# Normalising the second half's x in pieces during the first half, and giving its first column of h to the rounds of seven products

## The chip, the cores and the metric

One Trainium2 chip, one of its cores. The time is the device time of one execution in microseconds (us), as the median over several runs; the profile is of one execution, taken by the hardware profiler. Engines are called PE (TensorE: matmuls), PEld (its weight loads, which overlap), DVE (VectorE), ACT (ScalarE), POOL (GpSimd) and SP (SyncE, whose queue issues nearly all DMAs here).

## What is computed

x is 2048 tokens by 576 features. The reference normalises it, adds a spectral filter of it and a gated MLP with 4608 hidden columns:

```python
x = A_x
xn = _layernorm(x, axis=-1)
return x + _A_ref(xn, A_w_r, A_w_i) + _B_ref(xn, B_w_gate, B_w_up, B_w_down)
# _A_ref: irfft2(rfft2(xn) * (w_r + 1j * w_i))
# _B_ref: (sigmoid(xn @ w_gate) * (xn @ w_up)) @ w_down
```

All of it is fp32 in effect: each factor of a product is split into a high and a low part in the matmul format fp32r, and three of the four partial products are summed.

## The kernel before

**Halves and units.** The tokens are worked in two halves p = 0, 1 of 1024 tokens (two chunks of 512, or 8 tiles of 128). The hidden columns are worked in 36 blocks f of 128; unit u = 36p + f computes gate and value of block f for the tokens of its half. The first two units of each half (0, 1, 36, 37) are plain products, called in four calls by unit and chunk. All others use a scheme of seven products instead of eight: each product is 7 matmuls of 128x512 (`made`, L710) into the banks pA, pB and pE, from seven-scheme factors of x in the SBUF tensor `X` (A11, A12, A21, A22 and their sums S1 to S4) and factors of the weights in `w`. After a product into pE, DVE adds it to the value (`ys`, L814 for chunk 1, called y1 here, and L834 for chunk 0, y0) and multiplies by the gate (L836). The next product into the same bank waits for the first of these.

**The weights.** The first half reads the raw weights, makes sums and low parts of them (L282 on ACT; L284, L286, L306 to L309 on DVE) and spills seven sections per unit to DRAM (`wsp`). The second half reads them back, each section of 320 KB (L323) into the one place that the product of the unit before has just left, so a section has six products' time to land.

**h times w_down.** Two neighbouring blocks make a column j of h (18 columns). Of the two ways to multiply it, the plain one is `down` (L860, po): 12 matmuls of 128x288 for one tile, 8 tiles, so 96 for a column, then an addition to `acc` (L869). The other is the round (`seven`, L1071, ps): it takes two columns at once through seven items (factors `hs` of h, `wf` of w_down) of two steps with 12 matmuls of 128x288, so 168 a pair; its sums are L1005. A single column in a round is 84. `TWOS` lists which columns go through rounds: in the first half the pairs [2,3] to [14,15], in the second half the pairs [1,2] to [13,14], and [15] alone. Columns 0, 16 and 17 of the second half (0, 1, 16 and 17 of the first) are plain. A unit has seven turns; at each the next step of a round, or a `down`, and the side work is emitted. The eight `down`s of the second half's column 0 stand at turns 3 to 6 of unit 38 (`spots`), and the rounds of the second half begin at turn 5 of unit 41. From unit 39 on the spectral branch's passes are emitted there too (pd and others, L527 and on).

**The boundary.** Around units 34 to 37 x of the second half must be normalised into `X`. `second_pair` and `second_chunk_of_pair` read it transposed (`xg`), with rows of means and reciprocal deviations broadcast (`mr`), and `level` subtracts and multiplies on DVE (L1307, L1308); `second_factors` makes the sums of blocks (L1368); `put` writes high parts on ACT (L1357, L1358) and low parts on DVE (L1359, L1360) into `X`, where each factor may be overwritten only once the last unit of the first half has used it. The statistics come from `later_stats`, one tile in every fourth unit.

The order of instructions on each engine is set by a scheduler from the order of the code and its dependences; each engine then runs its own row in order, so an instruction that waits holds up all that stand behind it on its engine.

Of the kernel before, what the change touches and what calls it, by code (L numbers as in the profile page):

```python
# [16 lines left out]
P = 128  # L17
# [122 lines left out]
def _layout(x, w_r, w_i, w_gate, w_up, w_down):  # L140
# [10 lines left out]
    xg = x.reshape(NT, P, 2, HD)[TPP:, ..., ks].reshape(2, TPC, P, 2, KT + 1, P).transpose(0, 3, 5, 4, 1, 2).reshape(2, 2, P, (KT + 1) * CW)  # L151
# [12 lines left out]
def spectral_glu_kernel(ctx: ExitStack, tc: tile.TileContext, x, xt, xg, ri, w_in, w_down, out):  # L164
# [35 lines left out]
    rowd = tc.dram_tile([2, NT, P], F32, name="rowd")  # L200
# [142 lines left out]
    def parts_d(f):  # L343
        j, g = divmod(f, G)
        st, w = STD[j][:, g], flat(new_f((0, j, g), f"wd{f}"))
        placed(nc.scalar.activation(w[:, 0], st, AF.Copy))
        yield
        nc.vector.tensor_tensor(w[:, 1], st, f32(w[:, 0]), op=OP.subtract)
        if j not in SEVEN:
            nc.sync.dma_start(wdsp[f], f32(w).rearrange("p a d -> p (a d)"))  # L350
        else:
            for b in range(2):
                if (g, b) != (0, 1):
                    nc.sync.dma_start(fsp[j][:, WHERE[f"B{g + 1}{b + 1}"]], f32(w[:, :, b * HD:(b + 1) * HD]))
        yield
# [6 lines left out]

    def make_t(j):

        b = STD[j].rearrange("p g (b d) -> p (g b) d", b=2)
        t = R["pool"].tile([P, 4, HD], F32, tag="xa", name=f"wt{j}", bufs=TPC)
        nc.vector.tensor_tensor(t[:, 1:3], b[:, 1::2], b[:, :2], op=OP.subtract)
        yield
        nc.vector.tensor_tensor(t[:, 3], b[:, 3], t[:, 1], op=OP.subtract)
        nc.vector.tensor_tensor(t[:, 0], b[:, 2], t[:, 3], op=OP.subtract)  # L370
        yield
        th, tl = (R["pool"].tile([P, 4, HD], F32R, tag="xa", name=f"{k}{j}", bufs=TPC) for k in ("wth", "wtl"))
        nc.scalar.activation(th, t, AF.Copy)
        yield
        nc.vector.tensor_tensor(tl, t, f32(th), op=OP.subtract)
        for i, v in enumerate((th, tl)):
            nc.sync.dma_start(fsp[j][:, WHERE["T4"]:WHERE["T4"] + 4, i], f32(v))
        yield

    def make_dt(j):  # L380
# [9 lines left out]
        if j in SEVEN:  # L390
            yield from make_t(j)
# [451 lines left out]
    def down(p, j, m, together=True):  # L843
# [18 lines left out]
        def add():  # L862
# [91 lines left out]
    def split_rows(j, g):  # L954
# [7 lines left out]
        nc.sync.dma_start(wdsp[G * j + g].rearrange("p (a b d) -> p a b d", a=2, b=2), f32(w))  # L962

# [51 lines left out]
    def seven(p):  # L1015
# [9 lines left out]
        last = TWOS[p][-1] if p == 0 else TWOS[p][-2]  # L1025
# [34 lines left out]
        for i, (n, mm) in enumerate(steps):  # L1060
# [12 lines left out]
            slow = len(js) == 2 and js is not last  # L1073
# [256 lines left out]
    def load_whole(h):  # L1330
        t = R["pool"].tile([P, 4, 3, P], F32, tag="raw", name=f"xg1_{h}", bufs=2)
        t = t.rearrange("p b k f -> p (b k f)")
        nc.sync.dma_start(t, xg[1, h])
        WHOLE[h] = t = t.rearrange("p (k s) -> p k s", s=CW)
        XG[1, h], XGR[1, h] = t[:, :KT], t[:KR, KT]
# [247 lines left out]
```

## Time and profile before

| | us |
| --- | --- |
| median of 3 runs | 1370.13 (1370.08 to 1373.65) |
| profiled execution | 1369.23 |
| its span | 1367.4 |
| PE busy | 1356.0 (99%) |
| DVE busy | 1068.2 (78%) |
| ACT busy | 781.0 (57%) |

The span is from the first to the last instruction that the profiler records; the execution is 1.8 us longer than that. The busy times of the engines overlap. PE's granted clock is 1.00 nearly throughout, its higher level of 2.4 GHz. A matmul's own time in the trace is longer than the distance to the next one, since they are pipelined: a group of back-to-back matmuls is read by its length over its count.

### The profile page before, as it was taken

How to read it: one execution, taken by the hardware profiler on the slowest of the kernel's cores; microseconds unless marked ns; L12 is line 12 of the kernel's file. 1: busy time of each engine (PE TensorE's matmuls, PEld its weight loads, DVE VectorE, ACT ScalarE, POOL GpSimd, SP SyncE). 2: the span in 40 equal slices, each digit the busy share in tenths (PEclk: the TensorE clock that was granted, in tenths of full speed). 3: DMA queues.
4: the chain of work that ended last, by engine and by line, in shares of the span. 5: the costliest groups of instructions: out<-in, count | busy, mean ns of one | idle time of the engine just before them, and what ended most of it. 6: DMA issues, size and time to landing. Idle time of an engine off the chain costs nothing.

```text
span 1367.4 us, 20360 instructions
## 1 busy us (share of the span) xinstructions
PE 1356.0 (99%) x7656; PEld 1201.1 (88%) x7656; DVE 1068.2 (78%) x1555; ACT 781.0 (57%) x1228; POOL 3.3 (0%) x5
## 2 busy tenths in 40 slices
PE   8999999999999999999999999999999999999998
PEld 6888888888888888988888999988888888899887
DVE  7978988887878787999458768668777847777886
ACT  6644667676767677843236545447767634444442
POOL 0000000000000000000000000000000000000000
PEclk9999999999999999999999999999999999999999
DMA  7567877767676776585878887799898787775643
GB/s 260 210 227 279 301 292 267 275 262 273 263 268 263 276 264 267 206 311 184 302 246 267 267 252 249 215 307 314 301 311 304 241 282 243 239 232 178 200 150 87
DMA packets 127058, 346.56 MB, mean 253 GB/s; under 512 B 12816, under 2 KB 34096, under 8 KB 122224
## 3 DMA queue, kind: packets, MB, share of 16 engines
q1 hardware_dynamic: 125968, 343.94, 72.5%
q8 instruction: 61, 1.00, 0.3%
q10 hardware_dynamic: 992, 1.31, 0.3%
q14 instruction: 37, 0.30, 0.1%
HBM read 208.74 MB, written 136.46 MB: 252 GB/s over the span
## 4 chain that ended last, share of the span: by engine, by line
PE 95%; DVE 3%; issue 1%; ACT 0%; DMA 0%; DVEq 0%
PE pB L710 24%; PE ps L1071 24%; PE pE L710 17%; PE pA L710 16%; PE po L860 6%; PE pd L527 2%; PE pe L650 2%; PE pa L543 1%; PE pc L591 1%; PE py L619 1%; PE pb L566 1%; PE pz L632 0%; DVE w L284 0%; DVE X L477 0%; PE pg L710 0%
## 5 line engine op out<-in xcount | busy, mean ns | idle before, releaser
L710 PE MATMUL pB<-X,w 128*128 128x512 f32 x1484 | 374.9, 391 | 0.2 <-DVE X L477 0.2
L1071 PE MATMUL ps<-wf,hs 128*128 128x288 f32 x2436 | 358.6, 295 | 0.5 <-DVE acc L1005 0.4
L1071 PEld LDWEIGHTS ps<-wf,hs 128*128 128x128 f32 x2436 | 341.7, 188 | 14.9 <-ACT u L593 1.9
L710 PEld LDWEIGHTS pB<-X,w 128*128 128x128 f32 x1484 | 271.0, 188 | 49.1 <-DVE X L477 0.6
L710 PE MATMUL pE<-X,w 128*128 128x512 f32 x1064 | 265.3, 391 | 1.1 <-DVE ys L834 1.0
L710 PE MATMUL pA<-X,w 128*128 128x512 f32 (+1 forms) x1006 | 252.8, 389 | 0.7 <-DVE X L1359 0.3
L710 PEld LDWEIGHTS pE<-X,w 128*128 128x128 f32 x1064 | 194.1, 188 | 37.3 <-issue 1.4
L710 PEld LDWEIGHTS pA<-X,w 128*128 128x128 f32 x1006 | 182.6, 188 | 33.7 <-ACT X L476 0.7
L992 DVE TENSOR_TENSOR hs<-ys,hs 128x1024 fp32r<-128x1024 f32 (+1 forms) x105 | 124.7, 1187 | 35.8 <-ACT hs L989 34.4
L989 ACT ACTIVATE hs<-ys 128x1024 fp32r<-128x1024 f32 (+1 forms) x105 | 108.0, 1029 | 41.5 <-PE ps L1071 25.6
L282 ACT ACTIVATE w<-raw 128x768 fp32r<-128x768 f32 (+1 forms) x106 | 100.2, 948 | 25.7 <-DVE raw L306 8.6
L836 DVE TENSOR_TENSOR ys<-ys,g 128x1024 f32<-128x1024 f32 x67 | 81.9, 1223 | 3.6 <-DVE ys L834 0.5
L803 ACT ACTIVATE v<-pB 128x512 f32<-128x512 f32 x68 | 40.5, 596 | 76.2 <-PE pB L710 75.8
L284 DVE TENSOR_TENSOR w<-raw,w 128x512 fp32r<-128x512 f32 (+1 forms) x106 | 81.7, 771 | 2.9 <-ACT w L282 2.8
L817 ACT ACTIVATE g<-pB 128x512 f32<-128x512 f32 x68 | 40.6, 597 | 67.7 <-PE pB L710 67.3
L985 DVE TENSOR_TENSOR ys<-ys 128x1024 f32<-128x1024 f32 (+1 forms) x60 | 71.1, 1186 | 0.7
L860 PEld LDWEIGHTS po<-wb,hp 128*128 128x128 f32 x468 | 65.0, 188 | 3.0 <-DVE acc L869 0.4
L860 PE MATMUL po<-wb,hp 128*128 128x288 f32 x468 | 67.3, 295 | 0.0
L814 DVE TENSOR_TENSOR ys<-v,pE 128x512 f32<-128x512 f32 x68 | 46.5, 684 | 26.3 <-ACT v L809 26.0
L1005 DVE TENSOR_TENSOR acc<-acc,ps 128x576 f32<-128x576 f32 x55 | 41.2, 750 | 31.8 <-PE ps L1071 31.4
L834 DVE TENSOR_TENSOR ys<-v,pE 128x512 f32<-128x512 f32 x67 | 45.9, 684 | 23.6 <-PE pE L710 22.4
L869 DVE TENSOR_TENSOR acc<-acc,po 128x576 f32<-128x576 f32 x55 | 41.0, 751 | 23.9 <-PE po L860 23.7
(185 smaller groups left out, 1586.8 us busy)
## 6 DMA issues: line engine op xcount, KB each, us to landing
w<-wsp SPq DMA_DIRECT2D x246, 320.0 KB, 4.0
wsp<-w SPq DMA_DIRECT2D x34, 2240.0 KB, 6.8
wf<-fsp SPq DMA_DIRECT2D x105, 288.0 KB, 4.3
fsp<-wf SPq DMA_DIRECT2D x98, 288.0 KB, 3.4
raw<-in_w SPq DMA_DIRECT2D x34, 768.0 KB, 6.6
x<-sc SPq DMA_DIRECT2D x16, 580.0 KB, 5.5
ri<-in_ri SPq DMA_DIRECT2D x16, 580.0 KB, 5.6
dt<-in_wd SPq DMA_DIRECT2D x32, 288.0 KB, 5.2
```

Of the source, the lines that this page charges most:

```text
L282: placed(nc.scalar.activation(o[:, :, :3, :], src, AF.Copy))
L284: placed(nc.vector.tensor_tensor(o[:, :, 3:, :], src[:, :, :KT, :], f32(o[:, :, :KT, :]), op=OP.subtract))
L710: strictly(nc.tensor.matmul(bank[:, cols], w[:, sw, :], X[:, x, sx, cols], start=start and j == 0, stop=stop and j == len(steps) - 1, skip ...
L814: nc.vector.tensor_tensor(y1, v[:, 1], bank["E"], op=OP.add)
L834: nc.vector.tensor_tensor(place(u, 0), v[:, 0], bank["E"], op=OP.add)
L836: nc.vector.tensor_tensor(h, h, g, op=OP.mult)
L860: nc.tensor.matmul(pd[b], l, r, start=start, stop=stop)
L985: nc.vector.tensor_tensor(o, at(a), at(b), op=op)
L989: nc.scalar.activation(hs[:, :, 0], o, AF.Copy)
L992: nc.vector.tensor_tensor(hs[:, :, 1], o, f32(hs[:, :, 0]), op=OP.subtract)
L1005: nc.vector.tensor_tensor(o, a, b, op=op)
L1071: nc.tensor.matmul(pd[:, s], h[:, g, a, m], w[:, g, b], start=q == 0 and not seeded, stop=q == len(parts_) - 1, skip_group_check=seeded)
```

## The change

Three things are changed.

1. `TWOS[1]` is now [0,1] to [14,15], eight pairs. Column 0's `down`s in unit 38 and the lone [15] are gone; the rounds of the second half begin at turn 5 of unit 39. The factors of w_down for columns 0 and 1 that earlier came from `make_t` are made by `first_sums` in the second half's first units: it reads four pieces of w_down, sums them on DVE, splits four tiles `wt_T` on ACT and DVE and writes eight times 288 KB to `fsp`, from which the round reads them.
2. In the first half, 12 pieces of the second half's x (128 features of 4 x 128 tokens, 256 KB) are read in units 14 to 16, 18 to 20, 22 to 24 and 26 to 28. For each, `piece_level` issues four DVE instructions of 128x256 and `piece_sums`, a unit later, four of 128x128; the piece is written to the DRAM tensor `nsp` after each of the two. The statistics for it are moved to units 4 to 11, and one broadcast read per group of three pieces brings them in.
3. At the boundary the eight factors are read whole from `nsp` (`staged`, 768 KB each) and only `put` is left. The `acc` tiles of the second half are loaded at the turns of unit 38 (`new_acc`) instead of right after each spill.

The core of the diff:

```diff
+FIRST = LATE + 10
+SEVEN = range(NF // G - 2)
+PAIRED = [list(SEVEN[i:i + 2]) for i in range(0, len(SEVEN), 2)]
+TWOS = (PAIRED[1:], PAIRED)
...
-        if j in SEVEN:
-            yield from make_t(j)
...
-                    new_acc(1, m)
...
+    def first_sums():
+
+        js = TWOS[1][0]
+        for _ in range(4):
+            yield
+        for g in range(G):
+            load_raw_d(js, g)
+            yield
+        yield
+        yield
+        for i in range(2):
+            sums_d(js, i)
+            yield
+        sub_d(js, "T4", "B21", "T2", "B11")
+        for nm in ("T4", "T1", "T3", "T2"):
+            w = new_f((1, nm), f"wt_{nm}")
+            nc.scalar.activation(w[:, :, 0], d(js, nm), AF.Copy)
+            nc.vector.tensor_tensor(w[:, :, 1], d(js, nm), f32(w[:, :, 0]), op=OP.subtract)
+            for i, j in enumerate(js):
+                nc.sync.dma_start(fsp[j][:, WHERE[nm]], f32(w[:, i]))
+            yield
...
-        last = TWOS[p][-1] if p == 0 else TWOS[p][-2]
+        last = TWOS[p][-1]
...
-        for h in range(2):
-            level(0, XG[0, h])
-            yield
-            level(0, XGR[0, h])
-            yield
...
+    def piece_level(n):
+        v, b = ROWS2[n // (KT + 1)], PIECE[n]
+        for i, op in enumerate((OP.subtract, OP.mult)):
+            for c in range(2):
+                tc.keep_in_program_order(nc.vector.tensor_tensor(b[:, c], b[:, c], v[:, c, i].unsqueeze(1).to_broadcast([P, 2, P]), op=op))
+
+    def piece_sums(n):
+        A11, A12, A21, A22 = (PIECE[n][:, c, h] for c in range(2) for h in range(2))
+        for o, a, b, op in ((A22, A21, A22, OP.add), (A21, A11, A21, OP.subtract), (A11, A22, A11, OP.subtract), (A12, A12, A11, OP.subtract)):
+            tc.keep_in_program_order(nc.vector.tensor_tensor(o, a, b, op=op))
+
+    def piece_out(n, first):
+        m, k = divmod(n, KT + 1)
+        nc.sync.dma_start(nsp[first:first + 4, :, k, m * P:(m + 1) * P].rearrange("a p s -> p a s"),
+                          PIECE[n].rearrange("p c h s -> p (c h) s"))
...
+    def second_rows():
+
+        staged("A22", True)
+        yield
+        put("A11")
+        staged("S1")
...
-        both(A22, A21, A22, OP.add)
-        yield
-        put("S1", *A22)
...
+    for n in range(TPC * (KT + 1)):
+        q, r = divmod(n, 3)
+        u = FIRST + 4 * q + r
+        at, then = (u, (4, 4, 5)[r]), (u + 1, (4, 5, 6)[r])
+        for (u, i), f, *a in ((later_step(*at, -3), piece_in), (at, piece_level), (later_step(*at, 1), piece_out, 0),
+                              (then, piece_sums), (later_step(*then, 1), piece_out, 4)):
+            behind.setdefault((u, i), []).append(lambda f=f, n=n, a=a: f(n, *a))
...
+    for m in range(TPP):
+        extra.setdefault((NF + G + m // 7, m % 7), []).append(lambda m=m: new_acc(1, m))
...
-            if u == NF + G:
-
-                spots = {3: 2, 4: 2, 5: 2, 6: 2}
-            elif f == NF - 2:
+            if f == NF - 2:
...
-            if p == 0 and f and f % 4 == 0:
-                sides.append(later_stats(TPP + f // 4 - 1))
+            if LATE <= u < LATE + TPP:
+                sides.append(later_stats(TPP + u - LATE, (4, 5, 3, 4)[u % 4]))
```

What it does to the rows of the engines is shown at three places. First DVE in the first half, unit 26, from the adding of w_down pieces (dt) to the first weight work of the next unit; hs and wf are the factors of the round, ys<-v,pE the two additions y1 and y0. Before:

```order
L930 TENSOR_TENSOR dt<-dt 128x2x288
L814 TENSOR_TENSOR ys<-v_4155,pE_4157 128x512
L992 TENSOR_TENSOR hs_10_6_4304<-ys,hs_10_6_4304 128x2x512
L941 TENSOR_TENSOR wf_10_6_4306<-dt,wf_10_6_4306 128x2x288
L834 TENSOR_TENSOR ys<-v_4155,pE_4157 128x512
L930 TENSOR_TENSOR dt<-dt 128x2x288
L836 TENSOR_TENSOR ys<-ys,g_4154 128x2x512
L284 TENSOR_TENSOR w_4327<-raw_4308,w_4327 128x3x256
```

and after, with pc the piece and mr the statistics for it:

```order
L911 TENSOR_TENSOR dt<-dt 128x2x288
L796 TENSOR_TENSOR ys<-v_4297,pE_4299 128x512
L1314 TENSOR_TENSOR pc_4350<-pc_4350,mr_4347 128x256 x4
L997 TENSOR_TENSOR hs_10_6_4457<-ys,hs_10_6_4457 128x2x512
L922 TENSOR_TENSOR wf_10_6_4459<-dt,wf_10_6_4459 128x2x288
L816 TENSOR_TENSOR ys<-v_4297,pE_4299 128x512
L911 TENSOR_TENSOR dt<-dt 128x2x288
L818 TENSOR_TENSOR ys<-ys,g_4296 128x2x512
L287 TENSOR_TENSOR w_4480<-raw_4461,w_4480 128x3x256
```

The four instructions on a piece stand between y1 and the low part of hs; nothing else moved here.

Second, DVE at the boundary, from the last of the work on xg to y0 of unit 35. Before:

```order
L1307 TENSOR_TENSOR xg_1_5686<-xg_1_5686,mr_5683 128x1536
L961 TENSOR_TENSOR wb_17_0_5786<-dt,wb_17_0_5786 128x576
L1308 TENSOR_TENSOR xg_1_5686<-xg_1_5686,mr_5683 128x1536
L1359 TENSOR_TENSOR X<-xg_1_5506,X 128x1024
L1360 TENSOR_TENSOR X<-xgr,X 32x512
L814 TENSOR_TENSOR ys<-v_5689,pE_5691 128x512
L961 TENSOR_TENSOR wb_17_1_5796<-dt,wb_17_1_5796 128x576
L1359 TENSOR_TENSOR X<-xg_0_5509,X 128x1024
L1360 TENSOR_TENSOR X<-xg_0_5509,X 32x512
L1359 TENSOR_TENSOR X<-xg_1_5686,X 128x1024
L1360 TENSOR_TENSOR X<-xg_1_5686,X 32x512
L834 TENSOR_TENSOR ys<-v_5689,pE_5691 128x512
```

and after, where x_A are the factors read whole (A12, A21 and A22 in this order; that of S1 comes just ahead of the first row):

```order
L1341 TENSOR_TENSOR X<-x_A_5650,X 128x1024
L851 TENSOR_TENSOR acc<-acc,po_7_5890 128x576
L883 TENSOR_TENSOR hp_17_0_5903<-ys,hp_17_0_5903 128x512
L942 TENSOR_TENSOR wb_17_0_5916<-dt,wb_17_0_5916 128x576
L1342 TENSOR_TENSOR X<-x_A_5650,X 32x512
L796 TENSOR_TENSOR ys<-v_5821,pE_5823 128x512
L942 TENSOR_TENSOR wb_17_1_5928<-dt,wb_17_1_5928 128x576
L1341 TENSOR_TENSOR X<-x_A_5652,X 128x1024
L1342 TENSOR_TENSOR X<-x_A_5652,X 32x512
L1341 TENSOR_TENSOR X<-x_A_5818,X 128x1024
L1342 TENSOR_TENSOR X<-x_A_5818,X 32x512
L816 TENSOR_TENSOR ys<-v_5821,pE_5823 128x512
```

The instructions on xg (L1307, L1308) are gone, and y0 still stands behind the low parts of A21 and A22, which are now read from x_A.

Third, SP's queue around units 38 and 39. The loads of unit 39's weights are those from wsp_76 before and from wsp_77 after, those of unit 40 from wsp_77 and wsp_78. Before:

```order
L323 DMA w_6055<-wsp_75 128x640 x6
L323 DMA w_6055<-wsp_76 128x640
L172 DMA cf<-c_cf 128x2900
L323 DMA w_6055<-wsp_76 128x640 x4
L502 DMA xs_6364<-in_xt 128x768
L323 DMA w_6055<-wsp_77 128x640
L172 DMA am_6366<-c_am 128x512
L502 DMA xs_6413<-in_xt 128x768
L172 DMA am_6415<-c_am 128x512
L323 DMA w_6055<-wsp_76 128x640 x2
L968 DMA wf_1_0_6730<-fsp_145 128x576
L968 DMA wf_1_0_6730<-fsp_146 128x576
```

and after:

```order
L376 DMA acc<-in_x 128x576 x4
L326 DMA w_6178<-wsp_77 128x640
L966 DMA fsp_146<-wt_T_6304 128x576
L326 DMA w_6178<-wsp_77 128x640
L966 DMA fsp_147<-wt_T_6304 128x576
L326 DMA w_6178<-wsp_77 128x640 x2
L966 DMA fsp_146<-wt_T_6319 128x576
L966 DMA fsp_147<-wt_T_6319 128x576
L326 DMA w_6178<-wsp_77 128x640
L966 DMA fsp_146<-wt_T_6335 128x576
L966 DMA fsp_147<-wt_T_6335 128x576
L326 DMA w_6178<-wsp_77 128x640
```

Between the weights of unit 39 there are now eight writes of the factors of w_down, and four loads of acc stand ahead of them; the reads of wf by which the first round starts follow behind the weights of unit 40.

## Rows read from the trace of the kernel before

**Rows 1.** The page, part 1: busy us (share of the span) xinstructions of each engine.

```profile
PE 1356.0 (99%) x7656; PEld 1201.1 (88%) x7656; DVE 1068.2 (78%) x1555; ACT 781.0 (57%) x1228; POOL 3.3 (0%) x5
```

**Rows 2.** Waits of PE: us in total, times, longest us.

```profile
PE pE L710 <- DVE ys L834: 1.0, 1, 1.0
...
PE pA L710 <- DVE X L1359: 0.3, 1, 0.3
```

**Rows 3.** Windows: busy us (xinstructions) of each engine, clock, DMA share, GB/s.

```profile
100.00:600.00 500.00, 500.00 (x2740) 442.60 (x2739) 419.26 (x583) 344.31 (x507) 0.00 (x0) 1.00 0.72 271
600.00:640.00 40.00, 38.67 (x214) 33.44 (x213) 39.43 (x47) 14.98 (x23) 0.00 (x0) 1.00 0.56 210
660.00:680.00 20.00, 19.95 (x109) 17.32 (x108) 8.06 (x11) 4.67 (x9) 0.00 (x0) 1.00 0.92 352
680.00:700.00 20.00, 20.00 (x109) 17.58 (x108) 8.58 (x13) 4.87 (x8) 0.00 (x0) 1.00 0.65 202
720.00:1300.00 580.00, 579.92 (x3377) 519.37 (x3376) 431.64 (x605) 315.30 (x509) 0.00 (x0) 1.00 0.80 259
```

**Rows 4.** Chain of waits, long pieces: start us, us, what, xcount.

```profile
84.69 3.17 PE pE L710 x14
...
1354.02 7.88 PE po L860 x60
```

**Rows 5.** Timeline of PE at the boundary: start us, us, instruction [idle before <-releaser].

```profile
624.64 1.64 PE L710 MATMUL pA<-X,w 128*128 128x512 f32 x6 [0.30 <-DVE X L1359]
...
631.37 2.98 PE L710 MATMUL pE<-X,w 128*128 128x512 f32 x12 [1.02 <-DVE ys L834]
```

**Rows 6.** Timeline of DVE at the boundary, just before 631 us.

```profile
629.83 0.68 DVE L1360 TENSOR_TENSOR X<-xg,X 32x512 fp32r<-32x512 f32 x1
630.54 0.69 DVE L834 TENSOR_TENSOR ys<-v,pE 128x512 f32<-128x512 f32 x1
```

**Rows 7.** Timeline of ACT at the boundary.

```profile
615.13 1.06 ACT L1357 ACTIVATE X<-xg 128x1024 fp32r<-128x1024 f32 x1 [1.85 <-PE pA L710]
```

**Rows 8.** Lines of DVE by shape: busy us, mean ns of one | idle before.

```profile
L1368 DVE TENSOR_TENSOR xg<-xg,xg 128x1024 f32<-128x1024 f32 x4 | 4.9, 1220 | 0.0
...
L1307 DVE TENSOR_TENSOR xg<-xg,mr 128x1536 f32<-128x1536 f32 x2 | 3.5, 1756 | 0.0
...
L1307 DVE TENSOR_TENSOR xg<-xg,mr 128x1024 f32<-128x1024 f32 x2 | 2.4, 1220 | 0.0
...
L438 DVE TENSOR_TENSOR rm<-xa,rm 128x64 fp32r<-128x64 f32 x12 | 2.1, 220 | 0.1
...
L1307 DVE TENSOR_TENSOR xgr<-xgr,mr 96x512 f32<-96x512 f32 x2 | 1.4, 680 | 0.0
...
L370 DVE TENSOR_TENSOR wt<-std,wt 128x288 f32<-128x288 f32 x1 | 0.5, 458 | 0.0
```

**Rows 9.** Window of four units in the first half (columns as in rows 3).

```profile
408.70:475.30 66.60, 66.60 (x365) 58.95 (x364) 53.85 (x72) 47.49 (x70) 0.00 (x0) 1.00 0.69 266
```

**Rows 10.** Timeline of DVE in the first half, units 24 and 26.

```profile
408.71 0.75 DVE L1005 TENSOR_TENSOR acc<-acc,ps 128x576 f32<-128x576 f32 x1 [3.92 <-PE ps L1071]
...
422.39 0.68 DVE L814 TENSOR_TENSOR ys<-v,pE 128x512 f32<-128x512 f32 x1
...
454.50 0.68 DVE L814 TENSOR_TENSOR ys<-v,pE 128x512 f32<-128x512 f32 x1
457.94 1.23 DVE L992 TENSOR_TENSOR hs<-ys,hs 128x1024 fp32r<-128x1024 f32 x1 [2.76 <-ACT hs L989]
```

**Rows 11.** Timeline of PE in the first half, unit 24.

```profile
424.38 1.75 PE L710 MATMUL pE<-X,w 128*128 128x512 f32 x7
```

**Rows 12.** Windows of 5 us in units 38 and 39 (columns as in rows 3).

```profile
665.00:670.00 5.00, 5.00 (x24) 4.14 (x23) 0.53 (x1) 1.20 (x2) 0.00 (x0) 1.00 1.04 429
670.00:675.00 5.00, 5.00 (x35) 4.67 (x33) 2.20 (x3) 0.60 (x1) 0.00 (x0) 1.00 0.89 344
```

**Rows 13.** The page, part 6: DMA issues, KB each, median us to landing.

```profile
w<-wsp SPq DMA_DIRECT2D x246, 320.0 KB, 4.0
```

More of the change, by code (lines that the diff above doesn't have):

```diff
@@ L348, in parts_d @@
         nc.vector.tensor_tensor(w[:, 1], st, f32(w[:, 0]), op=OP.subtract)
[L349 to L354, printed above, removed]
+        for b in range(2):
+            if (g, b) != (0, 1):
+                nc.sync.dma_start(fsp[j][:, WHERE[f"B{g + 1}{b + 1}"]], f32(w[:, :, b * HD:(b + 1) * HD]))
         yield
@@ L404, in scales @@
         ts = slice(t0, t0 + n)
-        rs = pool.tile([P, 4, n], F32, tag="rs", name=f"rs{t0}", bufs=2)
+        rs = pool.tile([P, 4, n], F32, tag="rs", name=f"rs{t0}", bufs=2 if table else 1)
         ve, r0, w0, w1 = (rs[:, i] for i in range(4))
@@ L1072, in seven @@
                                      stop=q == len(parts_) - 1, skip_group_check=seeded)
-            slow = len(js) == 2 and js is not last
+            slow = js is not last
             if mm == 0:
@@ L1330, in load_whole @@
[L1330 to L1335, printed above, removed]
-    def second_chunk_of_pair():
-        load_rows(1)
-        load_whole(1)
+            nc.sync.dma_start(rowd.rearrange("t (i p) -> t i p", i=2), rows)
+    KEPT = {k: i for i, k in enumerate(("A11", "A12", "A21", "A22", "S2", "S4", "S3", "S1"))}
@@ L1362, in second_factors @@
-    def second_factors():
-        A11, A12, A21, A22 = ((XG[c, h], XGR[c, h]) for c in range(2) for h in range(2))
-        def both(o, a, b, op):
-            for i in range(2):
-                nc.vector.tensor_tensor(o[i], a[i], b[i], op=op)
-        both(A22, A21, A22, OP.add)
+        put("A22")
+        yield
+    def second_factors():
+        staged("S3", True)
+        put("S1")
+        staged("S4")
         yield
-        put("S1", *A22)
         yield
-        both(A21, A11, A21, OP.subtract)
+        put("S2")
@@ L1375, in second_factors @@
         yield
-        both(A11, A22, A11, OP.subtract)
         yield
-        put("S2", *A11)
-        yield
-        both(A12, A12, A11, OP.subtract)
-        yield
-        put("S4", *A12)
+        put("S4")
         yield
@@ L1451, in spectral_glu_kernel @@
             elif p and n == 2:
-                for g in range(G):
-                    load_rows_of(1, 0, g)
+                sides.append(first_sums())
             if p == 0 and n < 2:
@@ L1484, in spectral_glu_kernel @@
         late_input[0] = False
-        pend = [(p, 0, m) for m in range(0 if p else TPC, TPP)]
+        assert not (p and pend)
+        pend = [] if p else [(p, 0, m) for m in range(TPC, TPP)]
         for f in range(G, NF):
@@ L1542, in beside @@
                 turn(2 if u + 1 < NF else 1)
+                for a in behind.get((u, i), ()):
+                    a()
             unit(u, beside)
```

113 lines of the change are left out of this document (47 added, 66 removed).

## Prediction

> **What bounds the kernel now.** The first view is the page's part 1: PE is busy for 1356.0 of 1367.4 us, 99% [rows 1]. The second is the windows, to see whether that is so everywhere: PE is full from 100 to 600 us, loses 1.3 us between 600 and 640, 0.05 between 660 and 680, and 0.08 in the 580 us from 720 to 1300 [rows 3]. So the kernel is a row of matmuls with next to no holes, and only two things can make it shorter: fewer matmuls, or the hole around 600 to 640. The price of a matmul is its distance to the next one in a long group: 14 of 512 columns in 3.17 us, so 0.226 each, and 60 of 288 columns in 7.88, so 0.131 each [rows 4].
>
> The hole is read from the waits and the timelines. PE waits 1.02 us at 631.37 for y0 (L834) and 0.30 us at 624.64 for a low part of X (L1359) [rows 2, 5]. DVE ends one low part of X after another and reaches y0 at 630.54 with no idle time before it [rows 6]; in this window it is busy for 39.43 of 40 us [rows 3]. So here, and only here, DVE sets PE's time. Elsewhere it has room: 53.85 of 66.6 us in four units of the first half [rows 9].
>
> **Part 1: fewer matmuls.** Column 0's 96 `down` matmuls go, and the lone column 15 goes from 84 to its half of a pair. Before: 96 + 7 x 168 + 84 = 1356 matmuls of 128x288 for columns 0 to 15. After: 8 x 168 = 1344. That is 12 fewer, at 0.131 us: **-1.6 us**, all of it on the path, as PE is full there. It is certain as far as PE has its data in time.
>
> **Part 2: the boundary.** What leaves DVE there is L1307 and L1308, each 2 x 1756, 2 x 1220 and 2 x 680 ns, together 14.6 us, and the sums L1368, 4 x 1220 and 4 of 96x512, which I take as the same 680, so 7.6 us: 22 us in all [rows 8]. The order shows the last two of 1.75 us, 3.5 us, some ten rows ahead of y0, and in its length of 40 us the window had 0.6 us free [rows 3]. DVE then no longer runs behind, and y0 waits for its product alone. Its place in DVE's row is still behind the low parts of A21 and A22, but these wait for products of unit 35 that end before the product y0 needs. Of the 1.32 us [rows 5] I take all but nothing as left: **-1.3**, with bounds -0.3 (y0 late for another reason) and -1.3. Behind this hole nothing is late at once: in the following window, 660 to 680, PE loses 0.05 [rows 3].
>
> One thing could be late in its stead. On ACT the high part of S1 stands ahead of A12's, and S1's tile is read only after A11's tile is free. But ACT sat idle for 1.85 us until 615.13 for a product, since A12 may not be overwritten sooner [rows 7]; S1's copy of the same 1.06 us then pushes A12 to about 616.2, eight us before the 624.64 at which PE reads it. So I price this at nothing; the cover is gone if S1 lands after about 622.
>
> **Part 3: the pieces in the first half.** No row shows DVE on 128x256 or 128x128. 64 columns take 220 ns and 288 take 458 [rows 8], so 1.06 ns a column: 0.42 us for 256 and 0.29 for 128, between these two rows. A piece is then 4 x 0.42 + 4 x 0.29 = 2.9 us, twelve are 34 us, and three in four units are 8.6 us. Against that stand 66.6 - 53.85 = 12.7 us of idle time in four units [rows 9]: DVE goes from 81% to 94%. ACT gets nothing more, and no product waits for a piece by itself. The nearest deadline is where it counts. In unit 24, y1 ends at 422.39 + 0.68 = 423.07 and PE's next product into its bank starts at 424.38 [rows 10, 11]: 1.31 us of room. After the change two of the four small sums of a piece stand ahead of y1 in such a unit, 0.58 us, and the four on 256 columns stand behind it. In unit 26 these four, 1.7 us, stand between y1 and the low part of hs, where DVE had been idle for 2.76 us [rows 10]. So the added work falls into holes that it nearly fits, and DVE still has the 3.92 us before L1005 once in four units to catch up [rows 10]. I take **0** for this part, with 0 and +34 (all of it uncovered) as the bounds; since the room per four units is larger than the work, +2 is where I end the range for it. A gain is excluded: nothing there is removed but the few ops of `make_t`, in a stretch where PE waits for nothing of theirs. The 24 writes and 12 reads of 256 KB are 9.4 MB over some 240 us, 39 GB/s on top of 266 at a DMA share of 0.69 [rows 9], so room is left. On SP's queue each write waits for DVE, and the loads of w_down and of raw weights stand behind it; the raw ones are needed a unit later.
>
> **Part 4: units 38 to 40.** Here the change takes room away. Before, unit 38 was stretched by 96 x 0.131 = 12.6 us of `down`s, in which the queues emptied: 352 GB/s at a share of 0.92 from 660 to 680, then 202 at 0.65 [rows 3], together 11.1 MB in 40 us. After, the same loads have 27.4 us; to them come eight writes of 288 KB to `fsp`, 2.4 MB, and up to 1.2 MB of `acc` that were read earlier. That is 13.5 to 14.7 MB in 27.4 us, 490 to 540 GB/s, more than any window shows (429 from 665 to 670, 344 in the next [rows 12]). But not all of it is due by then: what must have landed for the first product of unit 40, about 22.3 us (14 products of 7 x 0.226) after the start of unit 38, is the eight `acc` at most, the weights of 39, `fsp`, the table cf of 1.5 MB and one section, 7.6 to 8.8 MB: 20 us at 429 GB/s and 22 to 26 at 344. A section has six products, 9.5 us, to land, and takes 4.0 [rows 13], so 5.5 us of lag are hidden. The direct price is 0 to +3.3 us, +5 if the lag grows through unit 40. I take **+0.5**, nearer the lower end, as 9.5 us stand against a lag of 0 to 4.
>
> The Trainium skill, DMA: Bandwidth & Descriptors, section Bandwidth, says that for transfers between HBM and SBUF a limit of some 358 GB/s per core binds. By that rule the 7.6 to 8.8 MB would take 21 to 25 us, an estimate, and the term would be some 0 to +2.5 us rather than 0.5. This trace's 429 GB/s in the window from 665 [rows 12] speaks against it as a limit for a core that runs alone.
>
> **Sum.** -1.6 - 1.3 + 0 + 0.5 = -2.4 us. Against the profiled execution's 1369.23 us that is 1366.8; that execution lies 0.9 us below the median of 1370.13, so in terms of the median **1367.7 us**, 0.18% less. A measurement of this kernel can tell about 0.3%, 4.1 us, from no change, so this is "within 0.3%": between 1366.0 and 1374.2.
>
> **Rivals.**
>
> *All holes close.* A matmul's own time in the trace is longer than its distance to the next, so holes of a few tenths of a us are not seen as idle time, and a DVE as full as in 600 to 640 may make some. If the matmuls' 1.6, the 1.3 and another 1.3 to 2.6 us of such holes all come, and units 38 to 40 cost nothing, the result is 1370.1 - 4.2 to -5.5, 1364.6 to 1366.0. For it speaks that DVE loses 22 us of work just ahead; against it that PE's waits name no more than two holes there [rows 2].
>
> *Weights late in units 38 to 40.* The lag exceeds 5.5 us, and PE waits at several sections: +2 to +6 instead of +0.5, so 1369.2 to 1373.2. It decides when the queues deliver less than about 300 GB/s there, which the window of 680 to 700 shows at light demand only. Against it: 344 and 429 [rows 12].
>
> *Slower: DVE sets the first half's time.* If the lag on DVE exceeds the 1.31 us ahead of y1, PE waits in each of 12 to 16 units. It decides at 0.7 us of lag beyond the two sums, for instance if the 256-column instructions with a broadcast operand take half as long again (4 x 0.63 = 2.5 us, 11 us in four units of 12.7 idle). At 0.5 us a unit that is 6 to 8 us, so 1374 to 1376, and more if SP's writes hold up the loads behind them. Against it: more than half of the added work stands behind y1, not ahead of it.
>
> *It does not do what it says at the boundary.* y0 still comes late behind A22's low part, which is in its old place: the 1.3 us stay, and the result is 1369.0. For it speaks the unchanged order of y0 and the low parts; against it that DVE arrives there with at least 3.5 us less in front of it.
>
> **How the numbers follow.** The forecast (1366.0 to 1368.8) has 0.52, the rival with all holes closed 0.20, that of the boundary 0.05, the late weights 0.09 (these and the forecast within 0.3%), and DVE in the first half 0.10; late weights and DVE together add 0.02 to slower, and gains that I do not see 0.02 to faster. Faster by over 0.3%: 0.22; within: 0.66; slower: 0.12. The range for 8 in 10 leaves out the lowest part of the first rival (0.05) and the slower cases (0.13 with the upper end of the late weights): 1364.8 to 1373.2.
>
> **What would show it.** Right: 12 fewer matmuls on PE (7644); PE without a wait for L834 or a low part of X between 600 and 640, and DVE there at some 65% instead of 99; DVE at 92 to 95% between 242 and 480 with PE still at 100%; the DMA share at 0.95 or more from 660 to 690 with PE's waits for a section under 1 us in all. Wrong: PE waits for y1, hs or w between 242 and 480 (part 3), for a section of w or for wf between 672 and 700 (part 4), or still for y0 at 631 (part 2). The prediction falls altogether if the loss in the first half comes to over 4 us, or if PE's distances between matmuls, not its waits, change.

## The result

The changed kernel takes **1372.77 us** (median of 22 runs, 1371.92 to 1373.96), the kernel before 1370.11 in runs beside it. The ratio is 1.0016, with a 95% interval of 1.0010 to 1.0022: some 0.2% slower. The forecast was 1367.7, that is 0.2% faster, with a range of 1364.8 to 1373.2. The time lies in the range and on the wrong side of no change.

The profiled execution after the change has a span of 1371.1 us. Part 1 of its page, to be read against [rows 1]:

```profile
PE 1357.4 (99%) x7644; PEld 1200.1 (88%) x7644; DVE 1076.0 (78%) x1623; ACT 783.5 (57%) x1227; POOL 3.3 (0%) x5
```

12 matmuls are gone, and yet PE is busy for 1.4 us longer in a span that is 3.7 us longer: a matmul's own time is longer than its distance to the next, so holes of a few tenths do not show as idle time. PE's waits (total, times, longest), against [rows 2]:

```profile
PE ps L1076 <- DVE acc L1010: 0.9, 2, 0.7
PE pB L691 <- ACT v L791: 0.7, 1, 0.7
PE pE L691 <- DMA w<-wsp: 0.6, 1, 0.6
PE pd L508 <- DVE x1l L246: 0.6, 2, 0.4
...
PE po L842 <- ACT hp L879: 0.5, 1, 0.5
```

The two waits of the boundary, for y0 and for a low part of X, are gone. Of these five the first stood at 0.4 us, once, in the kernel before; the other four are new. The windows, against [rows 3, 9] (busy time and count of PE, PEld, DVE, ACT, POOL, then clock, DMA share and GB/s):

```profile
408.70:475.30 66.60, 66.60 (x366) 58.95 (x365) 60.38 (x97) 47.38 (x70) 0.00 (x0) 1.00 0.82 305
600.00:640.00 40.00, 39.48 (x223) 34.67 (x222) 31.24 (x40) 18.01 (x28) 0.00 (x0) 1.00 0.81 299
680.00:700.00 20.00, 18.39 (x92) 14.37 (x91) 12.36 (x17) 8.13 (x14) 0.00 (x0) 1.00 0.98 376
```

DVE is down from 39.43 to 31.24 us of 40 at the boundary and up from 53.85 to 60.38 of 66.6 in the first half, where PE stays full. The new hole stands between 680 and 700 us: 1.6 us without PE, at a DMA share of 0.98.

**A ledger of losses.** To place the difference, I summed for each stretch the distance from one matmul's start to the next, less what it usually is for that many columns (0.227 us at 512, 0.132 at 288, 0.134 at 290, 0.120 at 256, 0.109 at 144, 0.108 at 128). All from the traces, in us; the last column is the median time of the runs:

| kernel | 0-60 | 60-200 | 600-660 | 660-745 | 745-860 | 860-900 | 1200-1320 | median |
| --- | --- | --- | --- | --- | --- | --- | --- | --- |
| before | 5.0 | 1.0 | 2.4 | 1.7 | 0.7 | 0.2 | 1.8 | 1370.1 |
| after | 5.8 | 1.5 | 1.2 | 3.8 | 0.6 | 1.6 | 3.0 | 1372.8 |
| e1 pieces only | 5.8 | 1.6 | 1.4 | 1.2 | 0.7 | 0.2 | 1.7 | 1369.1 |
| e2 column only | 5.0 | 1.1 | 2.3 | 3.7 | 0.7 | 1.6 | 3.1 | 1373.0 |
| e3 first pass later | 5.7 | 1.6 | 1.1 | 1.5 | 1.9 | 1.7 | 3.1 | 1371.9 |
| e4 T factors early | 5.5 | 1.2 | 1.8 | 0.3 | 0.7 | 1.6 | 3.1 | 1370.0 |
| e5 S2 behind hp | 6.3 | 1.5 | 1.1 | 3.9 | 0.7 | 1.6 | 3.1 | 1372.8 |
| e6 passes shifted | 5.3 | 1.6 | 1.1 | 4.4 | 0.8 | 0.5 | 1.5 | 1370.4 |
| e7 all three | 6.2 | 1.2 | 1.4 | 0.3 | 0.8 | 0.5 | 1.5 | 1366.8 |
| e8 before, shifted | 6.1 | 1.0 | 2.3 | 1.1 | 0.8 | 0.2 | 1.6 | 1370.1 |

Between 200 and 600 us all of these lose nothing. The stretches left out, 900 to 1200 us and the end, differ by 0.1 and 0.2 between before and after; in e6 and e7 the first of them loses 0.6 to 0.7 less than in the changed kernel. The first column differs by up to 1.1 us between kernels that begin with the same instructions: e8 begins as the kernel before does and has 6.1 against 5.0. From before to after the rest of the table is -1.6 (12 matmuls), +0.5, -1.2, +2.0, -0.1, +1.4 and +1.3, together +2.3, and the medians differ by 2.66.

### The profile page after: what moved, and what is told of

It reads as the page before. It is cut to its first block, busy times and chain, and to the rows that moved or that the text cites. A ratio compares the mean times of both kernels' runs of the same rounds, so it can differ in the third digit from the quotient of the medians.

```text
span 1371.1 us, 20481 instructions
## 1 busy us (share of the span) xinstructions
PE 1357.4 (99%) x7644; PEld 1200.1 (88%) x7644; DVE 1076.0 (78%) x1623; ACT 783.5 (57%) x1227; POOL 3.3 (0%) x5
## 4 chain that ended last, share of the span: by engine, by line
PE 90%; DVE 6%; ACT 2%; DMA 1%; issue 1%; SPq 0%; ACTq 0%; DVEq 0%
PE ps L1076 24%; PE pB L691 22%; PE pE L691 16%; PE pA L691 15%; PE po L842 4%; PE pd L508 2%; PE pe L631 1%; PE pc L572 1%; DMA w<-wsp 1%; PE py L600 1%; PE pa L524 1%; PE pb L547 1%; DVE w L287 1%; PE b L1152 1%; PE pz L613 0%
## 5 line engine op out<-in xcount | busy, mean ns | idle before, releaser
L1076 PE MATMUL ps<-wf,hs 128*128 128x288 f32 x2520 | 370.0, 296 | 0.9 <-DVE acc L1010 0.9
L1076 PEld LDWEIGHTS ps<-wf,hs 128*128 128x128 f32 x2520 | 353.1, 188 | 15.8 <-ACT u L574 1.9
L997 DVE TENSOR_TENSOR hs<-ys,hs 128x1024 fp32r<-128x1024 f32 x105 | 128.4, 1223 | 39.8 <-ACT hs L994 39.1
L994 ACT ACTIVATE hs<-ys 128x1024 fp32r<-128x1024 f32 x105 | 111.1, 1058 | 51.5 <-PE ps L1076 26.5
L818 DVE TENSOR_TENSOR ys<-ys,g 128x1024 f32<-128x1024 f32 x67 | 81.9, 1222 | 3.3
L785 ACT ACTIVATE v<-pB 128x512 f32<-128x512 f32 x68 | 40.5, 596 | 65.1 <-PE pB L691 64.6
L990 DVE TENSOR_TENSOR ys<-ys 128x1024 f32<-128x1024 f32 x60 | 73.1, 1218 | 0.6
L516 ACT ACTIVATE ah<-pd,rstd 64x290 fp32r<-64x290 f32 x64 | 31.9, 498 | 51.3 <-PE pd L508 34.4
L1010 DVE TENSOR_TENSOR acc<-acc,ps 128x576 f32<-128x576 f32 x55 | 41.2, 749 | 24.0 <-PE ps L1076 23.7
L791 ACT ACTIVATE v<-pB 128x512 f32<-128x512 f32 x68 | 40.4, 594 | 31.1 <-PE pB L691 30.7
L788 ACT ACTIVATE g<-pA 128x512 f32<-128x512 f32 x68 | 40.4, 594 | 27.2 <-PE pA L691 26.9
```

What stands on the lines that cost most here:

```text
L818: nc.vector.tensor_tensor(h, h, g, op=OP.mult)
L990: nc.vector.tensor_tensor(o, at(a), at(b), op=op)
L994: nc.scalar.activation(hs[:, :, 0], o, AF.Copy)
L997: nc.vector.tensor_tensor(hs[:, :, 1], o, f32(hs[:, :, 0]), op=OP.subtract)
L1010: nc.vector.tensor_tensor(o, a, b, op=op)
L1076: nc.tensor.matmul(pd[:, s], h[:, g, a, m], w[:, g, b], start=q == 0 and not seeded, stop=q == len(parts_) - 1, skip_group_check=seeded)
```

## The crowd on the queues in units 38 to 41

The windows of 5 us, against [rows 12]:

```profile
660.00:665.00 5.00, 5.00 (x24) 4.14 (x23) 3.49 (x5) 3.91 (x6) 0.00 (x0) 1.00 0.15 37
665.00:670.00 5.00, 5.00 (x24) 4.14 (x23) 1.11 (x2) 1.20 (x2) 0.00 (x0) 1.00 0.87 278
670.00:675.00 5.00, 4.98 (x23) 3.79 (x22) 1.36 (x2) 2.35 (x4) 0.00 (x0) 1.00 1.02 366
675.00:680.00 5.00, 5.00 (x24) 4.14 (x23) 3.13 (x3) 1.72 (x3) 0.00 (x0) 1.00 1.01 353
680.00:685.00 5.00, 4.31 (x19) 3.27 (x18) 0.69 (x1) 1.73 (x3) 0.00 (x0) 1.00 0.97 379
685.00:690.00 5.00, 4.34 (x18) 2.67 (x16) 3.61 (x5) 2.28 (x3) 0.00 (x0) 1.00 1.04 404
```

First the DMA engines stand nearly still (0.15 of their time), then they are full. SP's own timeline tells why, its issues before and after the still stretch:

```profile
653.29 2.07 SPq L376 DMA_DIRECT2D acc<-in_x  x4
663.75 0.33 SPq L326 DMA_DIRECT2D w<-wsp  x1
```

The last loads of acc are issued by 655, and the next instruction in SP's row is a section of unit 39's weights, which waits for the first product of unit 38 to leave its place. The chain of waits through this place (start us, length, what):

```profile
675.17 0.32 SPq L326
...
675.54 1.09 SPq L174
...
676.68 8.96 DMA w<-wsp
...
685.68 1.89 PE pA L691 x7
```

The first section of unit 40's weights (L326) follows on SP right behind the 1.45 MB of cf (L174). It is issued at 676.68 and takes 8.96 us to land, against 4.0 as the median [rows 13]; PE's product starts behind it, 0.2 us late. The timeline of PE shows what that does:

```profile
669.90 1.75 PE L691 MATMUL pA<-X,w 128*128 128x512 f32 x7
...
679.74 1.75 PE L691 MATMUL pB<-X,w 128*128 128x512 f32 x7
682.17 1.88 PE L691 MATMUL pB<-X,w 128*128 128x512 f32 x7 [0.69 <-ACT v L791]
...
688.18 1.88 PE L691 MATMUL pE<-X,w 128*128 128x512 f32 x7 [0.61 <-DMA w<-wsp]
```

The product at 669.90 is the first of unit 39; it ends at 671.65 and leaves the place for this section, which SP issues only 5.0 us later. The order on PE is another as well: two products into pB follow each other at 679.74 and 682.17, where in e3 and e4 below the first product of unit 40 stands between them, at 681.06 and 680.99. So PE waits 0.69 us for ACT to have read the first of the two, and unit 40 begins at 685.68.

**Experiments e1 and e2** part the change in two. In e1 the column is plain again:

```diff
-SEVEN = range(NF // G - 2)
-PAIRED = [list(SEVEN[i:i + 2]) for i in range(0, len(SEVEN), 2)]
-TWOS = (PAIRED[1:], PAIRED)
+SEVEN = range(1, NF // G - 2)
+TWOS = ([list(SEVEN[i:i + 2]) for i in range(1, len(SEVEN), 2)], [list(SEVEN[i:i + 2]) for i in range(0, len(SEVEN), 2)])
...
-                sides.append(first_sums())
+                for g in range(G):
+                    load_rows_of(1, 0, g)
```

> The changed kernel with the second half's column 0 plain again (eight down calls in unit 38, rounds [1,2] to [13,14] and [15] alone, T factors of column 1 made early, acc loaded after each spill); the pieces in the first half and the whole reads at the boundary stay. Theory queue (the loss of the change lies in units 38 to 41, where the first sums and the early rounds crowd the DMA queues): the boundary's gain stays and nothing is lost behind it, so 1368.5 to 1369.3, about 1.2 below the kernel before. Rival pieces (the pieces on DVE or their DMAs cost PE time): 1370.5 or more, with PE losing more than 0.5 us between 100 and 600 us.

Measured: 1369.05 us, ratio 0.9991 (0.9982 to 0.9999). The pieces alone are a small gain.

e2 is the other half, the kernel before with `TWOS`, `first_sums` and the acc loads of the changed one.

> The kernel before with only column 0 of the second half put into the rounds (first sums, rounds from unit 39, acc loaded in unit 38); x is normalised at the boundary as before. Theory queue: 12 matmuls fewer give -1.6, the loss between 660 and 745 us is 3.5 to 4 us instead of 1.7, and the losses of 2.5 us at 865 to 880 and 1245 to 1307 us come back as well, if they belong to the shifted rounds: 1372 to 1374. Rival pieces: the column alone gains its 1.6, so 1368.5.

Measured: 1373.04 us, ratio 1.0020 (1.0011 to 1.0029). The whole loss comes with the column (e1 and e2 against the kernel before are -1.1 and +2.9, together +1.9 where the change has +2.7; the intervals of some 1.2 either way cover that), and PE's waits repeat those of the changed kernel: 0.7 us for v, 0.6 for x1l and 0.5 for a section of weights.

**Experiment e3** takes bytes out of the crowd without touching the rounds:

```diff
-U1, U2, U3 = (0, 4.1), (76, 4.1), (151, 4.5)
+U1, U2, U3 = (7, 3.9), (76, 4.1), (151, 4.5)
...
-    begin[0] = [stage1]
+    begin[7] = [stage1]
```

> The changed kernel with the first pass of the spectral branch started seven turns later and then a little denser, so that the table cf, xs and am are loaded about 11 us later. Theory queue: 2.4 MB leave the crowded 670 to 697 us, PE's loss between 660 and 745 us falls from 3.8 to 1.5 or less; 1370.0 to 1371.0 unless the shifted passes lose something elsewhere. Rival order (the loss there comes from the order of the products and from ACT and DVE, not from what the queues carry): within 0.5 us of 1372.8.

Measured: 1371.88 us, ratio 1.0012 (1.0003 to 1.0021). The time misses both expectations. The loss of 660 to 745 us falls from 3.8 to 1.5, as the queue theory has it; 1.2 of that are lost again between 745 and 860, where the passes are now denser. Two of its windows:

```profile
660.00:665.00 5.00, 5.00 (x24) 4.14 (x23) 3.64 (x5) 3.91 (x6) 0.00 (x0) 1.00 0.09 20
...
680.00:685.00 5.00, 5.00 (x24) 4.14 (x23) 0.69 (x1) 1.44 (x3) 0.00 (x0) 1.00 0.95 321
```

The still stretch is there too, 20 GB/s at a share of 0.09, and yet PE has no hole behind it. The first section of unit 40 is issued at 675.28 and lands after 5.4 us, in time for the product at 681.06; cf is now loaded behind it:

```profile
686.39 0.42 SPq L174 DMA_DIRECT2D cf<-c_cf  x1
```

So the still stretch by itself is not what PE loses by.

**Experiment e4** takes out `first_sums` instead:

```diff
     def make_dt(j):
 
+        if j == 1:
+            yield from make_t(0)
...
+        if j == 1:
+            yield from make_t(j)
...
-            elif p and n == 2:
-                sides.append(first_sums())
```

> The changed kernel with the T factors of w_down for columns 0 and 1 made in the first half (as the kernel before made those of column 1), so the second half's first sums, their four reads and eight writes of 288 KB, are gone. Theory queue: 3.5 MB leave 655 to 680 us, PE's loss between 660 and 745 us falls from 3.8 to 1 to 1.5; up to 1 us is lost near 60 us, where DVE is the later engine: 1370.0 to 1371.2. Rival order: that loss stays above 3 us, 1372.5 or more.

Measured: 1370.00 us, ratio 0.9997 (0.9988 to 1.0006), 2.8 us below the changed kernel. The loss at 660 to 745 us is 0.3, less than that of the kernel before. Its windows where the changed kernel had its hole:

```profile
680.00:685.00 5.00, 5.00 (x24) 4.14 (x23) 2.63 (x5) 2.25 (x5) 0.00 (x0) 1.00 0.96 334
685.00:690.00 5.00, 5.00 (x32) 4.56 (x31) 2.79 (x5) 2.02 (x3) 0.00 (x0) 1.00 0.93 283
```

PE runs there without a hole, with the DMA engines busy for 0.93 to 0.96 of the time. The section is issued at 673.66 and lands after 3.3 us. And the early T factors cost nothing: the loss of 60 to 200 us is 1.2 against 1.5. So the crowd is the cause of 2.0 us of the loss, and e3 and e4 each mend it.

What in the crowd does it is less sure. e4 takes 3.5 MB out of the stretch, but with the first sums gone SP also issues cf 11 us earlier, well ahead of that section, as the kernel before does (664.04):

```profile
664.10 0.42 SPq L174 DMA_DIRECT2D cf<-c_cf  x1
```

e3 leaves the eight writes where they are, and only moves cf and what follows it. In each traced kernel with the hole, e2, e5 and e6 among them, cf stands just ahead of the first section of unit 40, at 674.9 to 675.7; before, e1 and e7 have it near 664 and no hole. So the place of 1.45 MB in the queue explains all these runs as well as the sum of the bytes does, and no run parts the two. Both experiments also take work off DVE and ACT here, the sums and splits of w_down or the first steps of the pass; that was not tried apart, and from 660 to 680 us of the changed kernel each of the two engines is busy for some 9 of 20 us.

## The rounds against the spectral passes

What e1 does not lose and e2 does is also the 1.4 us at 860 to 900 and 1.3 at 1200 to 1320 us. The timelines of DVE, and of PE behind it, at the first of these places in the changed kernel:

```profile
864.44 1.22 DVE L997 TENSOR_TENSOR hs<-ys,hs 128x1024 fp32r<-128x1024 f32 x1
865.58 0.76 DVE L246 TENSOR_TENSOR x1l<-pa,x1h 128x580 fp32r<-128x580 f32 x1
```

```profile
866.39 0.40 PE L508 MATMUL pd<-cf,fh 128*128 128x290 f32 x1 [0.39 <-DVE x1l L246]
```

PE's next pass (pd) waits for DVE to have read the one before (x1l, L246). ACT has the high part ready, but on DVE the low part of hs for the round (L997) stands ahead. The rounds begin 14 turns earlier than before, and each takes 28 turns for a pair, while the passes begin where they did: the work of both now meets on DVE at other turns. In the second stretch the longest wait is of the other kind, a step of the round behind DVE's addition to `acc` (L1010), which had 0.42 us before:

```profile
1307.01 1.88 PE L1076 MATMUL ps<-wf,hs 128*128 128x288 f32 x12 [0.68 <-DVE acc L1010]
```

The rest of the 1.3 us there was not read row by row.

**Experiments e6 and e8** shift the passes, in the changed kernel and in the one before:

```diff
-U1, U2, U3 = (0, 4.1), (76, 4.1), (151, 4.5)
+U1, U2, U3 = (0, 4.3), (77, 4.1), (152, 4.5)
```

> The changed kernel with the turns at which the spectral passes begin shifted against the rounds (first pass every 4.3 instead of 4.1 turns, second from turn 77, third from 152). Theory phase (the losses at 865 to 880 and 1245 to 1307 us come from where the rounds' steps now fall against these passes, so that DVE and ACT reach a pass's factor late): 1.4 us less lost between 860 and 900, 1 us less between 1200 and 1320, the crowd at 680 to 700 unchanged: 1370.2 to 1371.2. Rival load (DVE simply has too much work in the second half with one more pair in the rounds): the losses move but do not shrink, 1372.3 to 1373.3.

> The kernel before with the same shift of the spectral passes alone. Theory phase (the shift undoes what the earlier rounds did to the passes): nothing to gain here, 1370.1 to 1371.0. Rival (this shift is better for any such kernel): 1368.5 or less, and the comparison of the changed kernel would have to be made against this.

Measured: e6 1370.36 us, ratio 1.0002 (0.9993 to 1.0010), 2.4 below the changed kernel; e8 1370.06 us, ratio 1.0001 (0.9992 to 1.0010). The same shift is worth 2.4 us to the changed kernel and nothing to the one before. The window at the first place, of the changed kernel and then of e6:

```profile
860.00:900.00 40.00, 39.42 (x225) 34.62 (x224) 29.43 (x40) 17.84 (x27) 0.00 (x0) 1.00 0.73 228
```

```profile
860.00:900.00 40.00, 39.95 (x231) 35.83 (x230) 30.28 (x42) 19.64 (x31) 0.00 (x0) 1.00 0.73 215
```

DVE is no less busy with the shift (30.28 against 29.43 us) and PE has next to no idle time: that speaks for the place of its work and against its amount. e6 keeps the crowd at 660 to 745 us (4.4), as expected.

## The boundary

The forecast gain came: 2.4 us lost before, 1.2 after. What is left is a new wait, read from DVE, ACT and PE in turn:

```profile
624.67 1.22 DVE L1341 TENSOR_TENSOR X<-x_A,X 128x1024 fp32r<-128x1024 f32 x1
625.92 0.68 DVE L1342 TENSOR_TENSOR X<-x_A,X 32x512 fp32r<-32x512 f32 x1
626.64 0.69 DVE L816 TENSOR_TENSOR ys<-v,pE 128x512 f32<-128x512 f32 x1
...
628.07 1.23 DVE L818 TENSOR_TENSOR ys<-ys,g 128x1024 f32<-128x1024 f32 x1
```

```profile
627.48 1.06 ACT L1339 ACTIVATE X<-x_S 128x1024 fp32r<-128x1024 f32 x1 [2.81 <-DMA x_S<-nsp]
...
629.90 1.14 ACT L879 ACTIVATE hp<-ys 128x512 fp32r<-128x512 f32 x2
```

```profile
630.58 1.32 PE L842 MATMUL po<-wb,hp 128*128 128x288 f32 x8 [0.52 <-ACT hp L879]
```

ACT idles for 2.81 us for S2's read from DRAM, with the copy of hp (L879) behind it, for which PE waits at 630.58. **Experiment e5** asks whether that is the reason:

```diff
-        nc.scalar.activation(o[:, :KT], t[:, :KT], AF.Copy)
-        nc.scalar.activation(o[:KR, KT], t[:KR, KT], AF.Copy)
+        hold = tc.keep_in_program_order if k in ('S2', 'S4') else lambda i: i
+        hold(nc.scalar.activation(o[:, :KT], t[:, :KT], AF.Copy))
+        hold(nc.scalar.activation(o[:KR, KT], t[:KR, KT], AF.Copy))
```

> The changed kernel with the high parts of S2 and S4 held in program order on ACT, so that they stand behind the hp copies of column 17 at the boundary. Theory (the 0.7 to 1.2 us that PE still loses at 629 us come from ACT standing before S2's copy until its read from DRAM has landed): that wait goes and PE's loss between 600 and 660 us falls from 1.2 to about 0.5, 1372.0 to 1372.4. Rival (hp is late for another reason, its data): the loss stays, 1372.8.

Measured: 1372.82 us, ratio 1.0022 (1.0013 to 1.0030). My theory fell. S2 now stands behind hp, and the wait is what it was:

```profile
629.63 0.60 ACT L710 ACTIVATE g<-pA 128x512 f32<-128x512 f32 x1 [4.73 <-DVE ys L818]
630.13 1.14 ACT L879 ACTIVATE hp<-ys 128x512 fp32r<-128x512 f32 x2
```

```profile
630.80 1.92 PE L842 MATMUL po<-wb,hp 128*128 128x288 f32 x12 [0.50 <-ACT hp L879]
```

ACT now waits 4.73 us for L818, the product of y with its gate, which DVE reaches at 628.07 in the rows above (628.29 in e5) because y0 still comes behind the low parts of A21 and A22 (624.67 to 626.6) and L818 behind one of S1's. The idle time for S2 cost nothing, since hp's data came later still. That these low parts are what holds y0 is read from the rows; no experiment was made to move them. But in e4 the scheduler has put y0 ahead of those of A22:

```profile
624.37 0.69 DVE L837 TENSOR_TENSOR ys<-v,pE 128x512 f32<-128x512 f32 x1
```

```profile
627.57 1.06 ACT L1360 ACTIVATE X<-x_S 128x1024 fp32r<-128x1024 f32 x1 [2.62 <-DMA x_S<-nsp]
```

The product with the gate (L839 there) is then done at 628.16, and now S2 does stand in the way: ACT is at its high parts until 629.15, hp follows at 629.53, and PE, which comes to it earlier, waits 1.0 us instead of 0.5. So hp is held by DVE's order and by S2's read almost alike, and as far as these two traces show, mending one of the two alone gains nothing here.

## How much room DVE had in the first half

The pieces on DVE (mean ns behind the bar and comma) took what was estimated, 0.42 and 0.29 us:

```profile
L1314 DVE TENSOR_TENSOR pc<-pc,mr 128x256 f32<-128x256 f32 x48 | 17.1, 416 | 0.0
...
L1319 DVE TENSOR_TENSOR pc<-pc 128x128 f32<-128x128 f32 x48 | 13.8, 288 | 0.8
```

**Experiments e9 and e10** issue the four instructions of L1314 two and four times:

```diff
-        for i, op in enumerate((OP.subtract, OP.mult)):
+        for i, op in enumerate((OP.subtract, OP.mult) * 2):
+            i = i % 2
```

> The changed kernel with the four 128x256 instructions of each piece issued twice (so x of the second half is levelled twice and the output is not the reference's). They add 4 x 416 ns, 12 times, 20 us of DVE time, 5 us in four units whose DVE was busy for 60.4 of 66.6 us. Theory holes (the added work falls into idle time and behind the deadlines): PE's loss between 100 and 600 us stays at 0.7 and the time at 1372.8, within 0.6. Rival deadline (an extra 1.4 us ahead of the next product's addition is already too much): PE waits in each of the 12 units, 3 us or more slower.

> The changed kernel with the same four instructions issued four times (output not the reference's): 60 us of DVE time added, 15 us in four units against 6.2 us of idle time left. Theory holes: now DVE is over-full, PE waits between 240 and 500 us, 4 to 20 us slower than the changed kernel. Rival (DVE time in the first half does not matter at all): 1372.8.

Measured: e9 1372.93 us, e10 1389.44 us (ratio to before 1.0140, 1.0125 to 1.0155). The kernel before beside them took 1369.60, so e9 is 0.2% slower than it, as the changed kernel is. The window of four units, of e9 and of e10, and e10's longest waits behind the start:

```profile
408.70:475.30 66.60, 66.60 (x366) 58.96 (x366) 64.36 (x109) 47.53 (x70) 0.00 (x0) 1.00 0.84 304
```

```profile
408.70:475.30 66.60, 64.73 (x339) 54.74 (x339) 65.90 (x120) 44.88 (x67) 0.00 (x0) 1.00 0.80 285
```

```profile
PE pB L691 <- ACT v L785: 3.2, 4, 1.3
PE ps L1076 <- ACT hs L994: 1.5, 2, 0.8
PE pA L691 <- ACT g L788: 1.4, 3, 1.0
```

With DVE at 64.36 of 66.6 us PE is still full. At 65.90 it is not, and the waits then name ACT, which itself waits for DVE (7.1 us for y0 ahead of v, 6.7 us for L818 ahead of g): 16 us are lost between 200 and 600 us by the ledger's count (5.9 and 10.2). That added work falls into holes held up to 97% of DVE's time in this window.

## All three together

**Experiment e7** joins e4, e5 and e6.

> The changed kernel with all three mended: T factors of columns 0 and 1 made in the first half, S2 and S4 behind hp on ACT, and the spectral passes shifted. If the three causes are apart and add up: 1370.0 (T factors in the first half) less 0.8 and less 2.3, 1366.7 to 1367.6, some 3 below the kernel before; if they hide each other, 1368.5 or more.

Measured: **1366.84 us**, ratio 0.9977 (0.9968 to 0.9986), 3.2 us below the kernel before and 5.9 below the changed one. The single gains against the changed kernel, 2.8 and 2.4 (and nothing for e5), add up to 5.2, which the 5.9 meets within the intervals, so the two causes are apart. PE's waits, all but those of the start:

```profile
PE po L863 <- ACT hp L900: 0.4, 1, 0.4
...
PE pA L712 <- ACT X L478: 0.2, 1, 0.2
PE pE L712 <- DVE ys L817: 0.2, 1, 0.2
```

## Why the prediction was wrong

- **Part 1 (-1.6) was right.** 7644 matmuls, at the same distances.
- **Part 2 (-1.3) was right in size**, 1.2 by the ledger, but not in its mechanism. "DVE then no longer runs behind, and y0 waits for its product alone" did not come: DVE has no idle time there from 617.5 to 632 us, and y0 comes 2.5 us behind its product, still after the low parts of A21 and A22. PE no longer waits for it at its bank, and waits 0.5 us for hp instead. The case of S1 ahead of A12 on ACT, priced at nothing, cost nothing: A12's copy starts at 616.43 where 616.2 was worked out.
- **Part 3 (0) was right for the pieces**: the time on DVE, the holes and the deadline. A cost of 0.5 us at 132 us was left out. It is in e1 too, where a row waits for y1, after the statistics were moved to units 4 to 11; whether they cause it was not tried apart.
- **Part 4 (+0.5) was mis-sized: 2.0.** The direction was right, and the rival of late weights, +2 to +6, names the place. The step that failed is "A section has six products, 9.5 us, to land, and takes 4.0 [rows 13], so 5.5 us of lag are hidden". The 9.5 us run from 671.65, when the place for unit 40's first section is free. But SP issues that section only at 676.68: in its queue it stands behind the last section of unit 39, which waits for a product until 675.17, and behind cf, which the prediction counted in bytes but not in its place. It then takes 8.96 us. Together that is 14.0 us against 9.5. Bytes over a rate do not tell it: the 22.3 us from the start of unit 38 at 661.97 carried 298 GB/s, less than the 344 to 429 taken, but e4 carried 311 in the same time and PE was full.
- **A term is missing, and it turned the sign: the rounds against the passes, +2.7.** The prediction said which queue the earlier rounds crowd, and not what they meet on DVE and ACT for the 600 us after that. It took the loss of "0.08 in the 580 us from 720 to 1300" [rows 3] as a property of the stretch ("as PE is full there"), while it was one of that order. No part, rival or sign of it names this place; only its last sentence, on PE's distances between matmuls, would cover it.
- **Its signs.** 7644 matmuls, a full PE between 242 and 480 us and waits for a section under 1 us in all (0.6) came. DVE at the boundary was to be at 65% and is at 78; in the first half it was to be at 92 to 95% and is at 90; the DMA share from 660 to 690 us was to be 0.95 or more and is 0.84, with the still stretch in it.
- That the time lies within the range is luck. It is also within the 1369.2 to 1373.2 of the late weights, but the weights account for 2.0 us of it and the term that no one priced for 2.7.
- The rule of the Trainium skill (DMA: Bandwidth & Descriptors, Bandwidth) of some 358 GB/s per core had been weighed against 429 in one window. The full windows here, from 670 to 690 us, have 353 to 404, three of four above the rule, and the term it gave, 0 to 2.5 us, holds the 2.0. But what decided was not the rate, with or without that rule: it was that one section came late through its queue, while the DMA engines were as full in e3 and e4 without a hole.

With the terms as the ledger has them, -1.6 - 1.2 + 0.5 (at 132 us) + 2.0 + 2.7 is +2.4, where the medians show +2.66.

## What to carry to other kernels

When a change starts a periodic stream earlier, price its meeting with every other stream for as long as both run, and not only the start: here that cost more than the change could gain, and a shift of the other stream gave it back. A load is in time not when all bytes of a stretch fit, but when it is issued early enough: follow the one load that the next product needs through its queue, with the waits and the bytes that stand ahead of it, before dividing bytes by a rate. And an idle wait that ends just ahead of a late instruction proves nothing until that instruction's own data have been looked at.

## What I had not expected of the hardware

The very start differs between executions of the same instructions: e8 begins with the code of the kernel before, and loses 6.1 us in the first 60 where that loses 5.0; the other kernels lie between 5.0 and 6.3, those among them that begin with the same instructions too. The difference arises in the first 20 us, around the matmuls that only keep PE busy until x has come. A single span can't be compared more closely than by that 1 us. And a full DVE is not a late DVE: in e9 it was busy for 97% of four units with no wait of PE behind it.
